# An attention and two feed-forward layers on one core: layer 2 as seven products of quarter matrices, and a list schedule with other matmul lengths

## The chip, the cores and the metric

The kernel runs on one core of one Trainium2 chip. Its time is device time in microseconds (us) for one execution, the median of the runs of one session. The engines are TensorE (PE, with its weight loads as PEld), VectorE (DVE), ScalarE (ACT), GpSimd (POOL) and the queue of SyncE (SP), which issues every DMA of this kernel. The trace comes from one profiled execution.

## The reference

Causal attention with a compressive memory gives 2304 tokens of 512 numbers; two feed-forward layers follow. All data are 32-bit floats.

```
x = attention(q, k, v, M_prev, z_prev, beta)          # 4 batches, 8 heads, 576 tokens, 64 wide
h = x @ moe_w_in;   r = max(h, 0)                     # 2304 x 512 by 512 x 2048
x = (s * r * r + b) @ moe_w_out                       # layer 1
h = x @ moe2_w_in
g = max(h, 0) + alpha * min(h, 0)
y = g @ moe2_w_out                                    # layer 2, 2304 x 512 out
```

## The kernel before

Every matrix product of the two layers is made exact enough by splitting both operands into a high and a low part: three matmuls (high by high, high by low, low by high) stand for one. Tokens are the moving operand, in blocks of 512 or 256 columns; the weights are the stationary operand, 128 by 128 each. Layer 1 has a block of 512 and seven of 256 columns, layer 2 four of 512 and one of 256. For each of 16 slices `f` of the hidden width, `g1` makes the hidden slice (12 matmuls into the bank `hb`, in layer 2 also `sp` and `ob`), ACT and DVE apply the activation and split the result (`gr`), and `g2` adds it to the output (12 matmuls into the four banks `yb`). A block has 16 x 24 = 384 matmuls. `evac` carries the output banks to DRAM (`y1` for layer 1, `out_t` for layer 2), and `load_x` loads and splits the input of the next block.

The weights lie in DRAM as 8-byte words. `weights` loads 512 KB for each of 32 halves of a layer, and DVE makes floats of them (three instructions, L870, L873, L876), ACT casts the high part (L879), DVE subtracts for the low part (L882). The weights of layer 2 are made while the last block of layer 1 and the first of layer 2 run, in place of those of layer 1.

The order of all instructions is made when the program is built. `Plan.order` is a list scheduler: each operation has an engine, a duration and a priority, and the operation that can start first on its engine is placed next. The chip then runs each engine's instructions strictly in that order, and waits by semaphores. The durations are functions of the size, such as `t_r` for one matmul of the layers (L286), `t_p` for scores, `t_dve` and `t_act`. Attention has the higher priority on PE; the matmuls of layer 1 fill what it leaves, and after attention has ended layer 1 has PE to itself.

## Time and profile before

| | |
|---|---|
| median of 3 runs | 980.5 us (980.23 to 982.16) |
| profiled execution, its own time | 980.97 us |
| span of the profiled execution | 978.9 us |
| PE busy | 962.6 us, 98% of the span |
| DVE busy, ACT busy | 602.4 us (62%), 471.5 us (48%) |
| bytes moved by DMA | 93.22 MB, mean 95 GB/s |

The span goes from the first to the last instruction; the time of the execution is 2.07 us more. Busy time on PE is modelled at its end, so the spacing of the starts of matmuls tells more than the busy share. Stages follow one another: attention with layer 1 between its pieces to about 422 us, layer 1 alone to about 585 us, its last matmuls mixed with the first of layer 2, then layer 2.

### The profile page before, as it was taken

The numbers are of one execution on the slowest core, as the hardware profiler recorded it, in microseconds if no ns is written. First come the engines' busy times: TensorE is split into PE (matmuls) and PEld (weight loads), VectorE is DVE, ScalarE is ACT, GpSimd is POOL, SyncE is SP. The second block draws the span as 40 slices with busy tenths as digits, with TensorE's granted clock in tenths as the row PEclk, the third lists the DMA queues.
The fourth block names the chain that finished last, engine by engine and source line by source line (L and its number), as shares of the span: only waits on it lengthen the run. The fifth ranks groups of instructions, "written<-read, shape, count | busy, mean of one in ns | idle before, by whom it ended". The sixth has DMA issues, their size and how long they took to land.

```text
span 978.9 us, 18001 instructions
## 1 busy us (share of the span) xinstructions
PE 962.6 (98%) x7068; PEld 828.7 (85%) x7068; DVE 602.4 (62%) x1471; ACT 471.5 (48%) x1183; POOL 5.3 (1%) x29
## 2 busy tenths in 40 slices
PE   7999999999999999999999999999999999999998
PEld 5777777788888888999999998888888888888898
DVE  7999998677776766542122999945434443534344
ACT  7877766787787777645454663212112111211111
POOL 1000000000000000000000000000000000000000
PEclk9999999999999999999999999999999999999999
DMA  5359955465657555641000755502000200100010
GB/s 176 100 161 239 243 197 155 111 163 115 151 117 155 137 121 104 120 164 55 1 23 10 224 170 158 162 1 86 1 1 11 65 1 1 44 1 0 1 45 22
DMA packets 114693, 93.22 MB, mean 95 GB/s; under 512 B 83377, under 2 KB 94641, under 8 KB 114609
## 3 DMA queue, kind: packets, MB, share of 16 engines
q1 hardware_dynamic: 114608, 92.08, 34.8%
q8 instruction: 55, 0.90, 0.4%
q14 instruction: 30, 0.24, 0.1%
HBM read 59.29 MB, written 13.11 MB: 74 GB/s over the span
## 4 chain that ended last, share of the span: by engine, by line
PE 89%; DVE 5%; ACT 4%; issue 1%; DMA 0%; SPq 0%; ACTq 0%; DVEq 0%
PE yb L973 13%; PE yb L975 13%; PE yb L974 13%; PE hb L932 9%; PE hb L934 8%; PE hb L933 8%; PE sp L932 3%; PE sp L934 3%; PE sp L933 3%; PE ob L775 2%; PE ob L932 2%; PE ob L934 2%; PE ob L933 2%; PE sp L775 2%; PE yb L775 2%; PE sp L679 1%
## 5 line engine op out<-in xcount | busy, mean ns | idle before, releaser
L973 PE MATMUL yb<-gr,wt 128*128 128x256 f32 (+2 forms) x832 | 270.7, 325 | 0.7 <-ACT gr L954 0.5
L975 PE MATMUL yb<-gr,wt 128*128 128x256 f32 (+2 forms) x832 | 268.3, 322 | 0.0
L974 PE MATMUL yb<-gr,wt 128*128 128x256 f32 (+2 forms) x832 | 267.6, 322 | 0.0
L932 PE MATMUL hb<-xr,wt 128*128 128x256 f32 (+1 forms) x592 | 183.9, 311 | 5.3 <-ACT gt L946 3.7
L934 PE MATMUL hb<-xr,wt 128*128 128x256 f32 (+1 forms) x592 | 179.1, 303 | 0.3 <-DVE wt L882 0.3
L933 PE MATMUL hb<-xr,wt 128*128 128x256 f32 (+1 forms) x592 | 179.1, 303 | 0.0
L973 PEld LDWEIGHTS yb<-gr,wt 128*128 128x128 f32 x832 | 156.4, 188 | 17.1 <-issue 2.5
L975 PEld LDWEIGHTS yb<-gr,wt 128*128 128x128 f32 x832 | 157.1, 189 | 13.9 <-DVE gr L955 1.1
L974 PEld LDWEIGHTS yb<-gr,wt 128*128 128x128 f32 x832 | 156.5, 188 | 12.2
L955 DVE TENSOR_TENSOR gr<-gt,gr 128x256 fp32r<-128x256 f32 (+1 forms) x168 | 84.1, 501 | 126.8 <-ACT gr L954 126.4
L954 ACT CAST gr<-gt 128x256 fp32r<-128x256 f32 (+1 forms) x168 | 78.7, 468 | 143.3 <-DVE gt L952 136.1
L932 PEld LDWEIGHTS hb<-xr,wt 128*128 128x128 f32 x592 | 111.3, 188 | 18.2 <-ACT gt L946 6.1
L934 PEld LDWEIGHTS hb<-xr,wt 128*128 128x128 f32 x592 | 111.8, 189 | 5.8 <-DVE wt L882 0.7
L933 PEld LDWEIGHTS hb<-xr,wt 128*128 128x128 f32 x592 | 111.3, 188 | 4.5
L946 ACT ACTIVATE gt<-hb 128x256 f32<-128x256 f32 (+1 forms) x128 | 52.6, 411 | 98.2 <-PE hb L934 94.1
L954 ACT CAST gr<-mz 128x512 fp32r<-128x512 f32 (+1 forms) x40 | 23.2, 579 | 154.0 <-DVE mz L952 153.9
L932 PE MATMUL sp<-xr,wt 128*128 128x512 f32 (+1 forms) x160 | 58.8, 367 | 0.0
L933 PE MATMUL sp<-xr,wt 128*128 128x512 f32 (+1 forms) x160 | 58.8, 367 | 0.0
L934 PE MATMUL sp<-xr,wt 128*128 128x512 f32 (+1 forms) x160 | 58.8, 367 | 0.0
L947 ACT ACTIVATE gt<-gt 128x256 f32<-128x256 f32 (+1 forms) x128 | 57.1, 446 | 2.5
L955 DVE TENSOR_TENSOR gr<-mz,gr 128x512 fp32r<-128x512 f32 (+1 forms) x40 | 25.6, 639 | 25.1 <-ACT gr L954 25.1
L949 DVE TENSOR_SCALAR mz<-ob,alv 128x512 f32<-128x512 f32 (+1 forms) x20 | 14.0, 698 | 37.8 <-PE ob L934 37.6
(343 smaller groups left out, 1484.7 us busy)
## 6 DMA issues: line engine op xcount, KB each, us to landing
pool<-wout SPq DMA_DIRECT2D x18, 512.0 KB, 4.3
pool<-win SPq DMA_DIRECT2D x16, 512.0 KB, 4.1
room<-wout SPq DMA_DIRECT2D x14, 512.0 KB, 3.9
room<-win SPq DMA_DIRECT2D x13, 512.0 KB, 4.2
pool<-y SPq DMA_DIRECT2D x18, 256.0 KB, 4.4
out_t<-pool SPq DMA_DIRECT2D x16, 256.0 KB, 2.1
y<-pool SPq DMA_DIRECT2D x22, 128.0 KB, 1.8
pool<-kp SPq DMA_DIRECT2D x9, 288.0 KB, 4.0
```

The lines of the kernel that those rows point to most:

```text
L775: T.matmul(bank_at(bk)[rows, x:x + n], half(sqp, odd, q0, nq), half(sk, odd, k0, n), start=True, stop=True, skip_group_check=True)
L932: T.matmul(H_, W_h, X_h, start=(d == 0), stop=False)
L933: T.matmul(H_, W_h, X_l, start=False, stop=False)
L934: T.matmul(H_, W_l, X_h, start=False, stop=(d == KD - 1))
L946: op("ACT", t_act(n, 50), lambda: A.activation(out=t_, in_=H_, func=AF.Relu), r=[hk, "gr"], w=[tk], prio=-1)
L947: op("ACT", t_act(n), lambda: A.activation(out=t_, in_=t_, func=AF.Square), w=[tk], prio=-1)
L949: op("DVE", t_dve(n, 1.04, 60), lambda: V.tensor_scalar(out=t_, in0=H_, scalar1=0.0, scalar2=alv[:, f:f + 1], op0=ALU.min, op1=ALU.mult), ...
L954: op("ACT", t_act(n), lambda: A.copy(out=G_h, in_=t_), r=[tk], w=[("gh", gj)], prio=-1)
L955: op("DVE", t_dve(n), lambda: V.tensor_tensor(out=G_l, in0=t_, in1=G_h.bitcast(F32), op=ALU.subtract), r=[tk, ("gh", gj)], w=[("gl", gj)], ...
L973: T.matmul(Y, W_h, G_h, start=first, stop=False, skip_group_check=True)
L974: T.matmul(Y, W_l, G_h, start=False, stop=False, skip_group_check=True)
L975: T.matmul(Y, W_h, G_l, start=False, stop=False, skip_group_check=True)
```

## The change

Layer 2 alone gets other mathematics. Tokens are cut in two halves (`NTH` = 1152), the inner width of each product in two, the outer width in two, so that each product is two-by-two quarters. Seven products of sums and differences of quarters replace the eight products of quarters. Products are numbered 1 to 7 in the code. They need sums of weight quarters, made once, sums of input quarters, made for each block, and sums of results.

- `prepare` (L1061, 16 times) loads two 512 KB pieces of layer 2's weights, makes floats (L1077, L1080, L1082, each twice), makes four differences of 256 columns (L1087) and stores seven matrices to DRAM (`wd`, 512 KB and 384 KB, L1090). All this stands where layer 1 runs alone. The key "words" lets the two loads of one `prepare` start only when the floats of the one ahead are made.
- `fetch` (L1093) loads these matrices back into the places of layer 1's weights (L1108) and splits them on ACT and DVE (L1110, L1112): those of the first product from the last block of layer 1 on, those of the second in the last third of the first product.
- `hidden` makes layer 2's first product for all tokens: three blocks of 2 x 384 columns by eight groups, each group with seven products of 6 matmuls (L1236 to L1238), three copies out of PSUM (`copy_out`, ACT), three sums (`join`, DVE, L1251), four activations (`leak`: ACT, then DVE, L1263) and four stores of 192 KB to DRAM (`g1`).
- `output` loads `g1` back (L1338) and makes the second product: in each of three blocks, seven products of four chunks of 12 matmuls (L1366 to L1368). For each chunk the operand is summed where the product asks for it (`sub`, DVE, L1199) and split (`split`: ACT L1193, DVE L1194) into one of three buffers.
- The scheduler's `t_r` becomes 115.5 ns up to 256 columns and (n + 32) / 2.4 above, `t_p` changes a little, and a PE operation of the layers after one of attention is given 130 ns more, the other way round 90 ns.

```diff
-BLOCKS = {1: [(0, 512)] + [(t, 256) for t in range(512, NT, 256)],
-          2: [(t, min(512, NT - t)) for t in range(0, NT, 512)]}
+BLOCKS = [(0, 512)] + [(t, 256) for t in range(512, NT, 256)]
...
+NS, NTH = 384, NT // 2
+GATE = 8
+GROUPS = [(b, f) for b in range(NTH // NS) for f in range(8)]
...
             if e == "PE":
+                layer = prio >= 10 ** 7
+                dur += 0 if layer == self.layer else 130.0 if layer else 90.0
+                self.layer = layer
...
-    return max(108.0, n / 2.4 + 2.5)
+    return 115.5 if n <= NB else (n + 32) / 2.4
+def t_s(n):
+    return 6 * (n + 32) / 2.4
...
-    return 200 + sum(186 + 4 * n / 2.4 for n in ns)
+    return 206 + 4 * sum(ns) / 2.4 + (0, 0, 4, 160, 364)[len(ns)]
...
+            for x, f in enumerate((fa, fb)):
+                s = Slot(RES["pw"], size=2)
+                op("SP", 475, lambda s=s, x=x: nc.sync.dma_start(out=at(s, 1024, I32), in_=src[i, x]),
+                   r=[("x1", B - 1, NP - 1, 1), "words"], w=[s], bytes_=524288)
...
+                    out=o(), in0=words(s, 1), scalar=-0x40000000, in1=o(), op0=ALU.bitwise_and, op1=ALU.bitwise_or), r=[s], w=[f] + ["words"] * x)
...
+            for out, in0, in1 in (((fa, 512), (fb, 0), (fa, 0)), ((fa, 768), (fb, 256), (fa, 512)),
+                                  ((fb, 512), (fb, 256), (fb, 0)), ((fb, 768), (fa, 256), (fa, 768))):
+                op("DVE", t_dve(256), lambda out=out, in0=in0, in1=in1: V.tensor_tensor(
+                    out=q(*out), in0=q(*in0), in1=q(*in1), op=ALU.subtract), r=[fa, fb], w=[out[0]])
+            for x, (f, a, n) in enumerate(((fa, 0, 4), (fb, 256, 3))):
+                op("SP", 475, lambda f=f, a=a, x=x, n=n: nc.sync.dma_start(
+                    out=wd[key][:, i, x, 0:256 * n], in_=q(f, a, 256 * n)), r=[f], w=[("wd", key, i, x)], bytes_=131072 * n)
...
+        def fetch(key, i):
...
+                op("ACT", t_act(256 * n), lambda s=s, x=x, a=a, n=n: A.copy(out=wp(i, x)[:, a:a + n, 0, :], in_=fold(see(s))),
+                   r=s.keys, w=[("w2", i, x, a)], prio=-0.8 if key == "wi" else -0.5)
...
+        def split(src, dst, prio):
+            act(dst, t_act(2 * NS), lambda: A.copy(out=see(dst, F32R, 0, 2 * NS), in_=see(src)), r=src.keys, prio=prio)
+            op("DVE", t_dve(2 * NS), lambda: V.tensor_tensor(
+                out=see(dst, F32R, 2 * NS, 2 * NS), in0=see(src), in1=see(dst, F32, 0, 2 * NS), op=ALU.subtract),
+               r=src.keys, w=dst.keys, prio=prio)
...
+        def product(P, g, bank):
+            b, f = GROUPS[g]
+            def mm():
+                for k in range(2):
+                    X_h, X_l = (see(XP[P], F32R, 2 * NS * lo + NS * k, NS) for lo in range(2))
+                    W_h, W_l = (weight(P, f, lo, k) for lo in range(2))
+                    o = bank_of[bank][:, 0:NS]
+                    T.matmul(o, W_h, X_h, start=(k == 0 and P in (1, 5, 2)), stop=False, skip_group_check=True)
+                    T.matmul(o, W_h, X_l, start=False, stop=False, skip_group_check=True)
+                    T.matmul(o, W_l, X_h, start=False, stop=False, skip_group_check=True)
...
+            for g, (b, f) in enumerate(GROUPS):
+                al, be, ga = bk(g)
+                p1, u2, p5 = (SIDE[3 * (g % 2) + x] for x in range(3))
+                product(1, g, al)
+                copy_out(al, p1)
+                product(5, g, ga)
+                copy_out(ga, p5)
+                if g > 0:
+                    last(g - 1)
+                if f == 0:
+                    split(RAW[3], XP[4], -3 if b else -0.7)
+                product(6, g, al)
+                copy_out(al, u2)
+                product(3, g, ga)
+                c = pick(RING)
+                join(ga, u2, c)
+                leak(g, 1, c, None, c)
+                product(2, g, be)
+                c = pick(RING)
+                join(be, p1, c)
+                leak(g, 0, c, None, c)
+                product(7, g, al)
+                c = pick(RING)
+                join(al, p5, c)
+                leak(g, 3, c, None, c)
...
+        def output():
+            U = [quarter(q) for q in range(4)]
+            ring = [Buf("gr", 0, 4 * NS)] + [Buf("xr", 4 * NS * i, 4 * NS) for i in range(2)]
+            side = FREE + [Buf("poolx", 4 * NS + NS * i, NS) for i in range(7)] + SIDE[0:3]
...
+                for P in (4, 5, 1, 2, 6, 3, 7):
+                    bank = names[{1: "a", 6: "a", 7: "a", 2: "b", 5: "c", 3: "c", 4: "d"}[P]]
+                    for m in range(4):
+                        a11, a12, a21, a22 = (U[q][m] for q in range(4))
+                        if P == 5:
+                            sub(a22, a21, a22, None, ALU.add)
+                        elif P == 6:
...
+                        src = {4: a22, 5: a22, 6: a22, 1: a11, 2: a12, 3: a12, 7: a21}[P]
+                        dst = ring[count[0] % len(ring)]
+                        count[0] += 1
+                        split(src, dst, None)
+                        def mm(P=P, m=m, dst=dst, bank=bank):
+                            for e in range(2):
...
+                                for j in range(2):
+                                    W_h, W_l = (weight(P, 2 * m + e, lo, j) for lo in range(2))
+                                    o = bank_of[bank[j]][:, 0:NS]
+                                    T.matmul(o, W_h, G_h, start=(m == e == 0 and P in (1, 2, 4, 5)), stop=False, skip_group_check=True)
+                                    T.matmul(o, W_l, G_h, start=False, stop=False, skip_group_check=True)
+                                    T.matmul(o, W_h, G_l, start=False, stop=False, skip_group_check=True)
```

DVE in the second part of layer 1, before the change: `gr` is the split of the hidden slice (L955), `xr` the next block's input (L1046), `yb` the output bank (L1008). These rows cover a little more than one block.

```order
L955 TENSOR_TENSOR gr<-gt,gr 128x256
L1046 TENSOR_TENSOR xr<-pool,xr 128x256 x2
L955 TENSOR_TENSOR gr<-gt,gr 128x256 x15
L1008 TENSOR_SCALAR pool<-yb_96,sbv 128x256
L1046 TENSOR_TENSOR xr<-pool,xr 128x256 x2
L1008 TENSOR_SCALAR pool<-yb_97,sbv 128x256
L955 TENSOR_TENSOR gr<-gt,gr 128x256
```

DVE in the same part of the program after the change: one whole `prepare` and the start of the next (`pool` and `poolx` hold the words, the floats and the differences; L944 is what L955 was).

```order
L1077 TENSOR_SCALAR poolx<-pool 128x512
L1080 SCALAR_TENSOR_TENSOR poolx<-pool,poolx 128x512
L1082 SCALAR_TENSOR_TENSOR poolx<-pool,poolx 128x512
L1077 TENSOR_SCALAR pool<-poolx 128x512
L1080 SCALAR_TENSOR_TENSOR pool<-poolx,pool 128x512
L944 TENSOR_TENSOR gr<-gt,gr 128x256
L1082 SCALAR_TENSOR_TENSOR pool<-poolx,pool 128x512
L1087 TENSOR_TENSOR poolx<-pool,poolx 128x256 x2
L1087 TENSOR_TENSOR pool<-pool 128x256
L944 TENSOR_TENSOR gr<-gt,gr 128x256
L1087 TENSOR_TENSOR pool<-poolx 128x256
L1077 TENSOR_SCALAR pool<-poolx 128x512
```

Where DVE had fifteen splits in a row, each split now stands behind instructions of a `prepare` that wait for loads; 45 of L944 stand between the first L1077 and the last L1087.

DVE at the end of layer 2 before the change: three instructions for each hidden slice of 512 columns.

```order
L949 TENSOR_SCALAR gt<-sp_102,alv 128x512
L952 SCALAR_TENSOR_TENSOR gt<-sp_102,gt 128x512
L955 TENSOR_TENSOR gr<-gt,gr 128x512
L949 TENSOR_SCALAR mz<-ob,alv 128x512
L952 SCALAR_TENSOR_TENSOR mz<-ob,mz 128x512
```

DVE in `output` after the change, products 5 and 6 of the first block (`spare` and `poolu` are quarters, `xr` and `gr` the three buffers).

```order
L1199 TENSOR_TENSOR spare<-poolu,spare 128x768 x2
L1194 TENSOR_TENSOR xr<-spare,xr 128x768
L1199 TENSOR_TENSOR spare<-poolu,spare 128x768
L1194 TENSOR_TENSOR xr<-spare,xr 128x768
L1199 TENSOR_TENSOR spare<-poolu,spare 128x768
L1194 TENSOR_TENSOR gr<-spare,gr 128x768
L1199 TENSOR_TENSOR spare<-spare,poolu 128x768
L1194 TENSOR_TENSOR xr<-spare,xr 128x768
```

The sum of the next chunk (L1199) stands ahead of the subtraction of this one (L1194), and so in the time in which ACT casts.

## Rows read from the trace of the kernel before

**Rows 1.** The page: busy time of the engines, and the granted TensorE clock in 40 slices.

```profile
PE 962.6 (98%) x7068; PEld 828.7 (85%) x7068; DVE 602.4 (62%) x1471; ACT 471.5 (48%) x1183; POOL 5.3 (1%) x29
PEclk9999999999999999999999999999999999999999
```

**Rows 2.** All that PE waited for: line, releaser, us in total, times, longest.

```profile
PE sp L775 <- DMA room<-kp: 4.4, 1, 4.4
PE hb L932 <- ACT gt L946: 3.7, 6, 1.4
PE hb L932 <- DVE xr L704: 1.6, 1, 1.6
PE yb L573 <- ACT pool L741: 0.7, 2, 0.4
```

**Rows 3.** Two stretches: us, PE, PEld, DVE, ACT, POOL busy, clock, DMA share, GB/s.

```profile
422.00:585.00 163.00, 162.53 (x1383) 161.27 (x1382) 75.12 (x157) 85.48 (x208) 0.00 (x0) 1.00 0.31 95
669.00:756.00 87.00, 87.00 (x385) 72.04 (x384) 37.99 (x55) 13.54 (x22) 0.00 (x0) 1.00 0.07 25
```

**Rows 4.** ACT in order of time: copies from PSUM that end a block.

```profile
447.53 0.48 ACT L1003 ACTIVATE pool<-yb,sbv 128x256 f32<-128x256 f32 x1 [0.21 <-DVE pool L1008]
491.36 0.48 ACT L1003 ACTIVATE pool<-yb,sbv 128x256 f32<-128x256 f32 x1 [0.21 <-DVE pool L1008]
...
669.17 0.59 ACT L1006 COPY pool<-yb 128x512 f32<-128x512 f32 x1 [2.66 <-PE yb L975]
756.21 0.59 ACT L1006 COPY pool<-yb 128x512 f32<-128x512 f32 x1 [2.67 <-PE yb L975]
...
930.34 0.59 ACT L1006 COPY pool<-yb 128x512 f32<-128x512 f32 x1 [0.47 <-PE yb L975]
975.10 0.37 ACT L1006 COPY pool<-yb 128x256 f32<-128x256 f32 x1 [0.32 <-PE yb L975]
```

**Rows 5.** PE in order of time: first and last of eight matmuls of 258 columns.

```profile
535.77 0.28 PE L974 MATMUL yb<-gr,wt 128*128 128x258 f32 x1
...
536.62 0.28 PE L975 MATMUL yb<-gr,wt 128*128 128x258 f32 x1
```

**Rows 6.** Weight loads of layer 2 in 700 to 900 us, one of twelve groups.

```profile
L973 PEld LDWEIGHTS yb<-gr,wt 128*128 128x128 f32 x148 | 27.8, 188 | 5.7
```

**Rows 7.** SP: the first two 512 KB loads of layer 2's weights; their time to landing.

```profile
425.37 0.41 SPq L867 DMA_DIRECT2D pool<-win  x1
...
425.87 0.38 SPq L867 DMA_DIRECT2D pool<-wout  x1
...
DMA to landing us min/median/max: 4.0/4.6/5.2
```

**Rows 8.** The same for L867 loads of `wout` over the whole program.

```profile
DMA to landing us min/median/max: 3.5/4.2/6.6
```

**Rows 9.** Groups of DVE and ACT by shape: count, busy us, mean ns.

```profile
L870 DVE TENSOR_SCALAR pool<-pool 128x512 int32<-128x512 int32 x33 | 13.7, 422 | 0.0
L873 DVE SCALAR_TENSOR_TENSOR pool<-pool 128x512 int32<-128x512 int32 x33 | 22.7, 689 | 0.4
L955 DVE TENSOR_TENSOR gr<-gt,gr 128x256 fp32r<-128x256 f32 x120 | 50.9, 424 | 106.8 <-ACT gr L954 106.4
L955 DVE TENSOR_TENSOR gr<-gt,gr 128x512 fp32r<-128x512 f32 x48 | 33.2, 691 | 20.0 <-ACT gr L954 20.0
L954 ACT CAST gr<-gt 128x256 fp32r<-128x256 f32 x120 | 48.8, 406 | 19.5 <-DVE gt L952 16.9 <-PE yb L974 0.2
L954 ACT CAST gr<-gt 128x512 fp32r<-128x512 f32 x48 | 29.9, 623 | 123.8 <-DVE gt L952 119.1 <-PE yb L974 3.7 <-PE yb L975 1.0
```

**Rows 10.** The end: the last matmul and the last copy out of PSUM.

```profile
975.13 0.28 PE L975 MATMUL yb<-gr,wt 128*128 128x256 f32 x1
975.44 0.43 DVE L1012 COPY pool<-yb 128x256 f32<-128x256 f32 x1 [0.25 <-PE yb L975]
```

More of the change, by code (lines that the diff above doesn't have):

```diff
@@ L978, in g2 @@
                    w=[yk, ("g2", f)] + ([(yslot[d], "y")] if d in yslot else []),
-                   prio=MOE + cm["m"] + (1.5 if layer == 1 and n == NBIG else 0))
+                   prio=MOE + cm["m"] + (1.5 if n == NBIG else 0))
             cm["m"] += 1
@@ L1010, in evac @@
                        r=yr + ["sbv"], w=[s], prio=-2)
-                else:
-                    op("DVE", t_dve(n), lambda s=s, Y=Y: V.tensor_copy(out=at(s, n), in_=Y), r=yr, w=[s], prio=-2)
-                dst = (y1 if layer == 1 else outT)[:, d, t0:t0 + n]
+                dst = y1[:, d, t0:t0 + n]
                 op("SP", 475, lambda s=s, dst=dst: nc.sync.dma_start(out=dst, in_=at(s, n)), r=[s],
@@ L1035, in load_x @@
                 op("SP", 475, lambda xr=xr, src=src: nc.sync.dma_start(out=xr(), in_=src), r=rk,
-                   w=[s] + [("xset", x) for x in ((0, 1, 3) if xs == 3 else (xs,))], bytes_=512 * step * n,
-                   prio=-2 if layer == 2 and blk > 0 else None)
+                   w=[s, ("xset", xs)], bytes_=512 * step * n)
                 for e in range(step):
@@ new lines, in ready, with weight, __init__ @@
+        def ready(P, i):
+            x, a = PLACE[P]
+            return ("w2", i, x, 0 if x else a // 2 * 2)
+        def weight(P, i, lo, k):
+            x, a = PLACE[P]
+            return wp(i, x)[:, a, lo, k * 128:(k + 1) * 128]
+        class Buf:
+            def __init__(self, region, c0, n):
+                self.region, self.c0, self.n = region, c0, n
+                key = "pool" if region in ("poolr", "poolu") else region
+                self.keys = [(key, c) for c in range(c0 // 128, (c0 + n + 127) // 128)]
@@ new lines, in build, with hold @@
+        seen = set()
+        def hold(buf):
+            claim, extra = [], []
+            for k in buf.keys:
+                if k in seen:
+                    continue
+                seen.add(k)
+                region, c = k
+                lo, hi = 128 * c, 128 * c + 127
+                if region == "pool":
+                    claim += range(NSLOT - XS)
+                elif region == "poolx":
+                    o = NSLOT - XS
+                    claim += range(o + lo // GW, o + hi // GW + 1)
+                elif region == "xr":
+                    extra += [("xset", int(hi >= 2 * KD * NB))]
+                elif isinstance(region, int):
+                    extra += wkeys("wi", 2 * region + 1) + wkeys("wo", 2 * region + 1)
+                elif region in ("gr", "gt"):
+                    extra += [(x, j) for x in (("gh", "gl") if region == "gr" else ("gt",)) for j in range(2)]
+            return sorted(set(claim)), list(dict.fromkeys(extra))
@@ new lines, in build, with act @@
+        every = [("wd", key, i, x) for key in ("wi", "wo") for i in range(8) for x in range(2)]
+        def act(buf, dur, fn, r=(), prio=None, eng="ACT", extra_w=(), bytes_=0):
+            claim, extra = hold(buf)
+            op(eng, dur, fn, r=list(r) + (every if claim else []) + ([("g2", GATE)] if buf in XP.values() else []) + (
+                [("y1", len(BLOCKS) - 1, d) for d in range(KD)] if claim and max(claim) > NSLOT - XS + 4 else []),
+               w=buf.keys + extra + list(extra_w), prio=prio, claim=claim, bytes_=bytes_)
@@ new lines, in hidden, with last @@
+        def hidden():
+            op("DVE", 90, lambda: V.tensor_scalar(out=alm, in0=alv, scalar1=-1.0, scalar2=1.0, op0=ALU.mult, op1=ALU.add),
+               r=["alv"], w=["alm"])
+            inputs(0)
+            ng = len(GROUPS)
+            bk = lambda g: (("S0", "H", ("Y", 0))[g % 3], ("O", ("Y", 2))[g % 2], ("S1", ("Y", 1))[g % 2])
+            parts = {}
+            def last(g):
+                al = bk(g)[0]
+                product(4, g, al)
+                leak(g, 2, None, al, pick(RING))
+                if GROUPS[g][0] == NTH // NS - 1:
+                    fetch("wo", GROUPS[g][1])
+            for g, (b, f) in enumerate(GROUPS):
[23 more added lines that the diff above has]
+                leak(g, 3, c, None, c)
+                if f == 7 and g + 1 < ng:
+                    inputs(b + 1)
+            last(ng - 1)
@@ L1086, in build @@
         for b in range(B):
             attention(b)
-        for i, (layer, blk) in enumerate((l, j) for l in (1, 2) for j in range(len(BLOCKS[l]))):
-            moe(layer, blk, i % 2 if layer == 1 else 2 + blk % 2)
+        for key, src in (("wi", win2), ("wo", wout2)):
+            for i in range(8):
+                prepare(src, key, i)
+        for blk in range(len(BLOCKS)):
+            moe(blk, blk % 2)
         flush()
+        hidden()
+        output()
         order = plan.order()
```

339 lines of the change are left out of this document (223 added, 116 removed).

## The prediction

> **What bounds the kernel now.** I first read the page's shares: PE is busy for 98% of the span, DVE for 62%, ACT for 48%, and the granted clock is full (2.4 GHz) in all 40 slices [rows 1]. Then what PE waited for: 4.4 us for the first load, 3.7 us six times for ACT, little else [rows 2]. So PE is the bound throughout, and a change is worth what it takes off PE, if nobody else becomes the bound. Last the stages: while layer 1 runs alone, DVE is busy for 75 of 163 us and DMA for 0.31; in a block of layer 2 DVE for 38 of 87 us and DMA for 0.07 [rows 3]. There is room beside PE.
>
> What counts is the spacing of PE's matmuls, not their modelled length. Two copies at the same place of consecutive blocks of 512 columns are 87.04 us apart [rows 4], over 384 matmuls 226.7 ns each. Matmuls of 258 columns start 0.85 us apart over seven gaps, 121 ns [rows 5]. Both are columns plus 32 at 2.4 GHz (226.7 and 120.8 ns), which is what the diff writes into the scheduler. A block of 256 columns takes 43.83 us in layer 1, 114 ns each, and 44.76 us at the end of layer 2, 117 ns [rows 4].
>
> **What PE is given.** Layer 2 before: four blocks at 87.04 us and one at 44.76 us make 392.9 us. After, the order holds 1008 matmuls of `hidden` and 1008 of `output`, all of 384 columns, in place of 1920. No row shows 384 columns. By 258 and 512 it is 416 columns at 2.4 GHz, 173.3 ns; a straight line between 117 ns at 256 and 226.7 at 512 gives 172 ns. I take 173.3, since two shapes above 256 agree on it: 2016 x 173.3 = 349.4 us, with 346.8 us as the lower end. That is 43.5 us less. The copies and sums beside it lie on ACT and DVE.
>
> A rule of the Trainium skill (Perfetto Trace Analysis, "Identifying the Most-Contended Engine") speaks against it: TensorE's headroom is to be judged by the busy share of LDWEIGHTS, not of matmuls. A load is busy for 188 ns [rows 6]; 2016 of them, if they could not overlap, would be 379.0 us, and 13.9 us would be gained, not 43.5. This case's trace does not bear it out: at 258 columns matmuls and their loads follow each other every 121 ns.
>
> **What DVE and ACT are given.** Prices by shape [rows 9]: DVE takes 424 ns for 256 and 691 ns for 512 columns, so 0.56 us for 384 and 0.96 us for 768; ACT's cast takes 406 and 623 ns, so 0.51 and 0.84 us. A group of `hidden` is 42 matmuls, 7.28 us of PE. It gives DVE three sums and four activations, 3.9 us, and ACT three copies and four activations, 3.6 us. In the last eight groups the fetch of the second weights adds 2.3 us to DVE and 2.1 to ACT: 6.2 and 5.7 of 7.28 us. In `output` a chunk is 12 matmuls, 2.08 us. Its subtraction takes DVE 0.96 us, with a sum 1.92 us. Over a block that is 44 x 0.96 + 8 x 0.56 = 46.7 of 58.2 us; in products 6, 3 and 7, which all need sums, 12 x 1.92 + 2 x 0.56 = 24.2 of 25.0 us. DVE stays below PE everywhere, at the closest place by 3%.
>
> **Terms that can hold PE up.**
>
> *Preparing weights, beside layer 1.* The order puts each split of the hidden slice on DVE (L944) behind instructions that wait for loads. In the order 45 splits stand within the 16 `prepare`; PE needs 43.83 / 16 = 2.74 us for each, so 123.3 us or 7.7 us per `prepare`. The chain of one `prepare` runs from load to load: the second load is issued 0.5 us after the first and lands 5.2 us later (a pair in the trace, behind 256 KB of other data) [rows 7], then 0.42 + 2 x 0.69 = 1.8 us of DVE [rows 9], some 0.2 us of semaphores: 7.7 us, or 8.1 with a split of 0.42 us inside. If the chain is the slower one, PE is held through L944, which `g2` needs. 16 x 0.4 is 6 us, nothing is the other end; I take 3 us. With the longest landing, 6.6 us [rows 8], the chain takes 9.1 us and the loss is 22 us: a rival.
>
> *From layer 1 to layer 2.* The first products' operands are split in the last half of the last block of layer 1, beside `fetch`. From there DVE has 11 x 0.96 us for sums and splits, eight fetches at 2.3 us and eight splits of layer 1 at 0.42 us: 33 us of work, of which the later fetches are not urgent, in 22 us of half a block and 7 us of a first group. I take 2 us, between 0 and 8.
>
> *Two changes of token block in `hidden`.* Each gives DVE 10.6 us more, in the 16.6 us between the first operand's release and the last one's use, in which 8.9 us of its usual work fall. Two of the sums can come earlier, 17.6 remain. About 1 us each, 2 us in all (0 to 6).
>
> *The last eight groups and the start of `output`*: the load of the next quarter waits for `hidden` to end and takes about 4 us, then 3 us of sum, cast and subtraction; product 4, which needs no such load, gives 8.3 us of PE work as cover. 2 us (0 to 8).
>
> *The end.* Now the last copy starts at 975.44 and the last matmul ends at 975.41 [rows 10]; 3.5 us are left from there to the end of the span. After, four sums of 0.56 us stand in line on one engine, two of them just ahead of the last matmul's end: 1.4 us more.
>
> *Attention and layer 1 under the new lengths.* After its last attention matmul the order keeps 1485 matmuls, 2016 of them taken off 3501; before it was 3288 less 1920, 1368. So attention ends 117 matmuls or 13 us of PE work sooner, and `prepare` begins sooner. PE waited little there, apart from the first load, so there is little to win; jitter in a new order can cost as much. Zero, between -5 and +6 us.
>
> **Sum.** 978.9 - 392.9 + 349.4 + 1.4 + (3 + 2 + 2 + 2) = 945.8 us of span, 2.07 us more in time (980.97 less 978.9): 947.9 us. The profiled execution lies 0.5 us above the median of the runs shown, so I predict **947 us**, 3.4% less than 980.5.
>
> **Rivals.**
>
> *More is won* (934 us or less). PE has no wait in layer 2 and loses some waits of layer 1: 947 less the 9 us of waits, less 5 us. For it: layer 2 runs without a wait now. Against: every stall above is a new one.
>
> *Others pace PE* (960 to 980 us). The `prepare` chain with late landings (22 in place of 3 us: 966 us), or layer 2's engines pushed out of step, in 24 groups 1 us each, 24 in place of 4: 967 us. For it: DVE and ACT run in a fixed order made from durations (`t_dve(512)` is 0.60 us) below those of the rows (0.69 us). Against: average load is well below PE's.
>
> *Weight loads bound layer 2*: 947 + 29.6 = 977 us.
>
> *Slower than before: the chunks of `output` run as a chain.* If sum, cast and subtraction of a chunk don't overlap with the next chunk's, it takes 0.96 + 0.84 + 0.96 + 0.3 = 3.06 us against PE's 2.08 us. With sums in 16 of 28 chunks, three blocks: 48 x 0.98 = 47 us, 994 us. It decides from 2.8 us a chunk on (48 x 0.7 = 34 us). Against it: the order has the next sum ahead of this subtraction, and there are three buffers.
>
> **How the numbers follow.** Forecast, 935 to 959 us: 0.74. More won: 0.04. Others pace PE: 0.15. Weight loads: 0.02. Slower by a chain: 0.04. The remaining 0.01 is no change. About 0.2% is what a measurement can tell here: faster 0.95, same 0.01, slower 0.04. The range of 934 to 966 us takes in the forecast, its unknown ends and the nearer half of the paced cases.
>
> **What would show it.** In the trace after: matmuls of 384 columns 173 ns apart; layer 2 some 355 us from its first to its last matmul; all waits of PE on DVE and ACT in layer 2 below some 8 us; L944 near its old rhythm of 2.74 us while L1077 runs; the last attention matmul near 409 us. The prediction is wrong if the spacing at 384 columns is 188 ns, if PE waits on L1194 chunk by chunk, if L944 comes late behind L1082, or if attention takes longer in its new order.

## The result, and the profile after

| | before | after |
|---|---|---|
| median of 4 runs each, one session | 980.92 us (980.23 to 982.16) | 941.03 us (938.19 to 942.06) |
| profiled execution, its own time | 980.97 us | 942.04 us |
| span of the profiled execution | 978.9 us | 940.0 us |

The ratio is 0.9587, with a 95% interval of 0.9562 to 0.9613: 4.1% less, where 3.4% was predicted. The predicted 947 us is 6 us too high and the range of 934 to 966 us holds the time.

First the page of the changed kernel, busy time and granted clock, which answers to [rows 1]. PE is as full as before, with DVE at 76% where it was at 62%.

```profile
PE 920.5 (98%) x7164; PEld 843.0 (90%) x7164; DVE 715.5 (76%) x1636; ACT 604.4 (64%) x1413; POOL 5.3 (1%) x29
...
PEclk9999999999999999999999999999999999999999
```

What PE waited for in the changed kernel, to be read beside [rows 2]. The three rows on L1368, L964 and L1236 are the new stalls; L796 and L928 are old ones under new line numbers.

```profile
PE sp L796 <- DMA room<-kp: 4.6, 1, 4.6
PE hb L928 <- ACT gt L941: 2.4, 3, 1.5
PE yb L1368 <- DVE xr L1194: 1.3, 1, 1.3
PE yb L964 <- DVE gr L944: 1.0, 5, 0.3
...
PE sp L1236 <- ACT waste L1248: 0.5, 1, 0.5
```

The stages (columns as in [rows 3]): the second part of layer 1, where `prepare` runs, then `hidden` without its first groups, then `output`.

```profile
422.00:536.00 114.00, 113.63 (x987) 113.24 (x986) 88.03 (x194) 53.43 (x136) 0.00 (x0) 1.00 0.78 274
...
590.00:760.80 170.80, 169.82 (x973) 168.00 (x972) 130.61 (x220) 109.36 (x217) 0.00 (x0) 1.00 0.54 175
760.80:935.50 174.70, 173.27 (x998) 172.61 (x996) 129.78 (x154) 78.38 (x106) 0.00 (x0) 1.00 0.41 125
```

DVE and the DMA queue are far busier than before: 0.78 of DMA in 422 to 536 us, where [rows 3] has 0.31. PE is still idle for about 1 us only in `hidden` and 1.4 us in `output`.

PE in order of time, from the changed kernel: two matmuls 24 apart in layer 1, the one long wait of `output`, two matmuls 59 apart at 384 columns (59 x 173.2 ns), and the last one.

```profile
464.42 0.28 PE L928 MATMUL hb<-xr,wt 128*128 128x256 f32 x1
...
467.14 0.28 PE L928 MATMUL hb<-xr,wt 128*128 128x256 f32 x1
...
769.46 0.34 PE L1367 MATMUL yb<-xr,wp 128*128 128x384 f32 x1
771.12 0.44 PE L1368 MATMUL yb<-xr,wp 128*128 128x384 f32 x1 [1.32 <-DVE xr L1194]
...
839.72 0.33 PE L1367 MATMUL sp<-xr,wp 128*128 128x384 f32 x1
...
849.94 0.33 PE L1366 MATMUL ob<-xr,wp 128*128 128x384 f32 x1
...
935.05 0.34 PE L1368 MATMUL sp<-xr,wp 128*128 128x384 f32 x1
```

ACT's copies at the ends of layer 1's blocks, which answer to [rows 4] (447.53 and 491.36 there).

```profile
447.21 0.46 ACT L991 ACTIVATE pool<-yb,sbv 128x256 f32<-128x256 f32 x1
...
491.20 0.46 ACT L991 ACTIVATE pool<-yb,sbv 128x256 f32<-128x256 f32 x1
...
536.24 0.48 ACT L991 ACTIVATE poolx<-yb,sbv 128x256 f32<-128x256 f32 x1
```

So the blocks of layer 1 end where they did, with all of `prepare` beside them: a block takes 43.99 us where it took 43.83. From the copy at 536.24 us to the end of the span it is 403.8 us; before it was 442.6 us (978.9 less 536.28, the same copy of before). All of the gain lies there.

The weight loads of `hidden` and `output`, one of many groups, as in [rows 6]: 188 ns each.

```profile
L1236 PEld LDWEIGHTS yb<-poolr,wp 128*128 128x128 f32 x96 | 18.0, 188 | 0.6 <-DVE poolx L1251 0.6
```

DVE in order of time: a sum of `output` that waits for a load, with the three instructions behind it, and the sums at the end.

```profile
769.24 0.96 DVE L1199 TENSOR_TENSOR spare<-poolu,spare 128x768 f32<-128x768 f32 x1 [1.88 <-DMA poolu<-g]
770.11 0.95 DVE L1194 TENSOR_TENSOR xr<-spare,xr 128x768 fp32r<-128x768 f32 x1
770.98 0.95 DVE L1199 TENSOR_TENSOR spare<-poolu,spare 128x768 f32<-128x768 f32 x1
771.85 0.95 DVE L1194 TENSOR_TENSOR gr<-spare,gr 128x768 fp32r<-128x768 f32 x1
...
934.90 1.02 DVE L1251 TENSOR_TENSOR gr<-sp,waste 128x384 f32<-128x384 f32 x2 [4.07 <-PE sp L1368]
935.84 0.55 DVE L1251 TENSOR_TENSOR gt<-sp,waste 128x384 f32<-128x384 f32 x1
936.30 0.55 DVE L1251 TENSOR_TENSOR waste<-sp,waste 128x384 f32<-128x384 f32 x1
```

Two things are to be seen here. The first four are 0.95 us long but start 0.87 us apart: independent DVE instructions overlap by 0.08 us. And from the last matmul's end (935.39 us) to the end of the span it is 4.6 us, where it was 3.5 us.

### The profile page after: what moved, and what is told of

It reads as the page before. It is cut to its first block, busy times and chain, and to the rows that moved or that the text cites. A ratio compares the mean times of both kernels' runs of the same rounds, so it can differ in the third digit from the quotient of the medians.

```text
span 940.0 us, 19297 instructions
## 1 busy us (share of the span) xinstructions
PE 920.5 (98%) x7164; PEld 843.0 (90%) x7164; DVE 715.5 (76%) x1636; ACT 604.4 (64%) x1413; POOL 5.3 (1%) x29
## 4 chain that ended last, share of the span: by engine, by line
PE 74%; DVE 13%; ACT 5%; DMA 5%; issue 2%; SPq 0%; DVEq 0%; ACTq 0%
PE yb L962 6%; PE yb L964 5%; PE hb L928 5%; PE yb L963 5%; PE hb L929 5%; PE hb L930 5%; PE sp L1368 3%; PE sp L1367 3%; PE sp L1366 3%; PE yb L1368 2%; PE yb L1367 2%; PE yb L1366 2%; PE yb L1236 2%; PE yb L1238 2%; PE yb L1237 2%
## 5 line engine op out<-in xcount | busy, mean ns | idle before, releaser
L928 PE MATMUL hb<-xr,wt 128*128 128x256 f32 (+1 forms) x512 | 152.5, 298 | 2.5 <-ACT gt L941 2.4
L962 PE MATMUL yb<-gr,wt 128*128 128x256 f32 (+2 forms) x512 | 154.1, 301 | 0.7 <-ACT gr L943 0.5
L964 PE MATMUL yb<-gr,wt 128*128 128x256 f32 (+2 forms) x512 | 151.2, 295 | 1.0 <-DVE gr L944 1.0
L930 PE MATMUL hb<-xr,wt 128*128 128x256 f32 (+1 forms) x512 | 149.4, 292 | 0.3 <-DVE wt L894 0.3
L929 PE MATMUL hb<-xr,wt 128*128 128x256 f32 (+1 forms) x512 | 149.3, 292 | 0.0
L928 PEld LDWEIGHTS hb<-xr,wt 128*128 128x128 f32 x512 | 96.3, 188 | 11.6 <-issue 4.4
L962 PEld LDWEIGHTS yb<-gr,wt 128*128 128x128 f32 x512 | 96.4, 188 | 9.1 <-issue 3.7
L964 PEld LDWEIGHTS yb<-gr,wt 128*128 128x128 f32 x512 | 96.6, 189 | 5.9 <-DVE gr L944 2.9
L944 DVE TENSOR_TENSOR gr<-gt,gr 128x256 fp32r<-128x256 f32 (+1 forms) x128 | 58.3, 456 | 56.2 <-ACT gr L943 53.7
L930 PEld LDWEIGHTS hb<-xr,wt 128*128 128x128 f32 x512 | 96.4, 188 | 3.5 <-DVE wt L894 0.7
L929 PEld LDWEIGHTS hb<-xr,wt 128*128 128x128 f32 x512 | 96.2, 188 | 2.1
L963 PE MATMUL yb<-gr,wt 128*128 128x256 f32 (+2 forms) x320 | 93.6, 292 | 0.0
L963 PEld LDWEIGHTS yb<-gr,wt 128*128 128x128 f32 x320 | 60.3, 188 | 1.2
L963 PE MATMUL yb<-gr,wu 128*128 128x256 f32 (+2 forms) x192 | 56.2, 292 | 0.0
L1262 ACT ACTIVATE waste<-poolx 128x384 f32<-128x384 f32 x48 | 25.2, 525 | 26.2 <-DVE poolx L1251 26.1
L1193 ACT CAST xr<-spare 128x768 fp32r<-128x768 f32 x30 | 25.0, 835 | 24.7 <-PE sp L1367 7.5
L963 PEld LDWEIGHTS yb<-gr,wu 128*128 128x128 f32 x192 | 36.2, 188 | 0.9
L1193 ACT CAST xr<-poolu 128x768 fp32r<-128x768 f32 x24 | 20.1, 838 | 25.1 <-PE sp L1367 13.8
L1236 PE MATMUL yb<-poolr,wp 128*128 128x384 f32 x104 | 35.0, 336 | 0.4 <-DVE poolx L1251 0.3
```

The source lines that it names most:

```text
L928: T.matmul(H_, W_h, X_h, start=(d == 0), stop=False)
L929: T.matmul(H_, W_h, X_l, start=False, stop=False)
L930: T.matmul(H_, W_l, X_h, start=False, stop=(d == KD - 1))
L944: op("DVE", t_dve(n), lambda: V.tensor_tensor(out=G_l, in0=t_, in1=G_h.bitcast(F32), op=ALU.subtract), r=[tk, ("gh", gj)], w=[("gl", gj)], ...
L962: T.matmul(Y, W_h, G_h, start=first, stop=False, skip_group_check=True)
L963: T.matmul(Y, W_l, G_h, start=False, stop=False, skip_group_check=True)
```

## The experiments

The theory to be tested: PE's columns make the gain, the new work stays beside PE, the lengths of the schedule are worth nothing. The rivals: the lengths give a part; DVE, the chain of `prepare` or the chunks of `output` pace PE; weight loads bound it. Each time below is a median beside the kernel before (980.5 to 981.8 us in the three sessions), with the ratio's 95% interval; the changed kernel's ratio is 0.9587.

### The lengths of the schedule

**All old, in the changed kernel.**

```diff
-                layer = prio >= 10 ** 7
-                dur += 0 if layer == self.layer else 130.0 if layer else 90.0
-                self.layer = layer
...
-    return 115.5 if n <= NB else (n + 32) / 2.4
+    return max(108.0, n / 2.4 + 2.5)
...
-    return 6 * (n + 32) / 2.4
+    return 6 * (n / 2.4 + 2.5)
...
-    return 206 + 4 * sum(ns) / 2.4 + (0, 0, 4, 160, 364)[len(ns)]
+    return 200 + sum(186 + 4 * n / 2.4 for n in ns)
```

> The changed kernel, scheduled with the old lengths of matmuls and no price for a change of kind; its work is the same. My theory: the gain is the columns that PE no longer has in layer 2, the lengths are worth nothing, so 941 us with 3 us either way, and attention still ends near 408 us, since layer 1's place among the pieces of attention is set by how many matmuls fit. Rival: the lengths brought a part of the 40 us, because DVE and ACT are given an order that PE's real pace upsets: then 947 us or more, with waits of PE on DVE or ACT of several us that the changed kernel does not have.

954.4 us (0.9713 to 0.9753). My theory fell, the rival's number came. The copy that ended layer 1's block 6 at 536.24 us starts at 542.14 us, and in the first group of layer 2 PE has one wait of 7.5 us on L1260, which is L1263 under other numbers.

**New lengths alone, in the kernel before.** The same edits, the other way round, without layer 2's products.

> The kernel before, with the new lengths and prices of changes alone. My theory: 981 us with 3 us either way. Rival (the lengths give a part of the gain by themselves): 976 us or less. If the lengths only help where the new layer 2 has a dense order on DVE and ACT, this run shows nothing and the run with the old lengths in the changed kernel does.

985.72 us (1.0043 to 1.0069), 5 us slower than before, with block 6's copy at 543.97 us. So the lengths are no better in themselves. They help only in the changed kernel, and two more runs asked which of them.

**Only the products' length old.**

```diff
-    return 6 * (n + 32) / 2.4
+    return 6 * (n / 2.4 + 2.5)
```

> The changed kernel with only the length of layer 2's own products put back to the old form (162.5 in place of 173.3 ns a matmul). The run with all lengths old was 13 us slower than the changed kernel: 6 us by the end of layer 1 and one wait of 7.5 us in the first group of layer 2, where DVE had the splits of fetched weights (L1112) ahead of an activation (L1263). In this kernel's order those splits still stand ahead of the first group, as in the changed kernel. My theory now: the lengths of layer 1 and of scores set how far the loads and splits are when layer 2 begins, and the length of layer 2's products does not matter: 941 us with 3 us either way. Rival (the products' own length makes the wait): 947 to 950 us, with a wait of several us on L1263.

939.64 us (0.9562 to 0.9596), no wait above 1 us in layer 2.

**Only the lengths of layer 1 and of scores old**, and no price for changes of kind.

```diff
-                layer = prio >= 10 ** 7
+                layer = False
...
-    return 115.5 if n <= NB else (n + 32) / 2.4
+    return max(108.0, n / 2.4 + 2.5)
...
-    return 206 + 4 * sum(ns) / 2.4 + (0, 0, 4, 160, 364)[len(ns)]
+    return 200 + sum(186 + 4 * n / 2.4 for n in ns)
```

> The other half: the changed kernel with the old lengths of layer 1's matmuls and of scores and no price for changes of kind, the products of layer 2 at their new length. Its order has ten splits of fetched weights behind the first sums of the first group, as in the run with all lengths old. My theory: the whole 13 us are here, block 6 of layer 1 ends near 542 us, PE waits some 7 us on L1263 in the first group and the granted clock falls behind it: 954 us with 3 us either way. Rival: 947 us or less.

954.84 us (0.9719 to 0.9758): the whole difference is here. DVE of this run in the first groups of layer 2 (L1112 splits fetched weights, L1263 is the activation of product 4):

```profile
611.23 0.96 DVE L1112 TENSOR_TENSOR wp<-poolx,wp 128x768 fp32r<-128x768 f32 x1 [2.00 <-ACT wp L1110]
612.50 1.35 DVE L1112 TENSOR_TENSOR wp<-poolx,wp 128x512 fp32r<-128x512 f32 x2 [0.32 <-ACT wp L1110]
613.89 0.61 DVE L1263 SCALAR_TENSOR_TENSOR poolx<-poolx,alm,sp 128x384 f32<-128x384 f32 x1
```

PE at the same place:

```profile
608.65 0.34 PE L1238 MATMUL ob<-poolr,wp 128*128 128x384 f32 x1
614.56 0.69 PE L1236 MATMUL sp<-xr,wp 128*128 128x384 f32 x1 [5.57 <-DVE poolx L1263]
```

And the stages of this run around it (columns as in [rows 3]):

```profile
609.00:617.00 8.00, 2.29 (x6) 1.78 (x6) 3.74 (x6) 3.24 (x5) 0.00 (x0) 0.78 0.63 205
617.00:625.00 8.00, 6.97 (x25) 6.98 (x26) 7.36 (x14) 5.25 (x12) 0.00 (x0) 0.58 0.35 124
```

DVE reaches the splits of weights that are just being fetched, waits for them, and the activation that frees PE's bank stands behind them. PE starts 31 matmuls in 16 us where 92 fit: 5.7 us are idle, and the granted clock is 0.58 in the 8 us that follow. In the changed kernel all but one of the 24 splits stand ahead of the first sums of layer 2 (L1251), beside layer 1; here eleven stand behind them.

What moved them is the end of attention, since `prepare` waits for its last output, and the fetch of the first product's weights for the last store of `prepare`. Here are the first loads of `prepare` (L1074) and all of these fetches (L1108) with the times of the first and the last start, ahead of the dots in the changed kernel, behind them in this run:

```profile
L1074 SPq DMA_DIRECT2D pool<-win x10: 332/429/838, 409.5 to 463.0; - x10
L1108 SPq DMA_DIRECT2D poolx<-wdwi x24: 319/320/531, 544.0 to 592.9; - x24
...
L1074 SPq DMA_DIRECT2D poolx<-win x5: 345/383/923, 424.0 to 472.0; - x5
L1108 SPq DMA_DIRECT2D poolx<-wdwi x24: 319/320/829, 564.8 to 613.2; - x24
```

The fetch begins 20.8 us later, though the last matmul of layer 1 starts only 3.9 us later. Of the 20.8 us, 6.3 are a longer `prepare`, and the rest is attention, whose last matmul starts at 422.7 us in place of 408.3. Behind it 1404 matmuls of layer 1 are left here and 1485 in the changed kernel: the planner, which with the old lengths takes 109 in place of 115.5 ns for one, set 81 more, some 9 us, among the pieces of attention. The numbers left go the same way elsewhere: 1368 in the kernel before and 1482 in it with the new lengths, and 1509 in the next run, where 117 in place of 115.5 ns is all that changes. The other 5 us are waits of PE at L594, which transposes the rows of attention's softmax: 5.5 us in all in the first 64 us, where the changed kernel has 0.4 us. The longest:

```profile
PE yb L594 <- ACT room L579: 2.1, 1, 2.1
```

By spans, 4.7 us are lost by block 6's copy (540.94 us), about what these waits take, and 7.8 us behind it. Which of the three (matmuls, scores, changes of kind) does how much of it was not tried, though the next run shows that the length of the matmuls alone moves the number left; nor is it known why the old lengths make the planner's order wait at L594.

**A length 1.5 ns longer.**

```diff
-    return 115.5 if n <= NB else (n + 32) / 2.4
+    return 117.0 if n <= NB else (n + 32) / 2.4
```

> The changed kernel with 117.0 in place of 115.5 ns for a matmul of up to 256 columns, both within what the trace shows (113 to 118). My theory: the place of attention's end and of layer 1's blocks moves by a few us with any change of these numbers, without a sense of direction (block 6 ended at 536.3, 544.0, 542.1 and 536.2 us in the kernel before, in it with the new lengths, in the changed kernel with the old ones, and in the changed kernel): 938 to 949 us, with the difference at block 6's end, and no wait of several us in layer 2. Rival (the better the length, the better the order, so that 1.5 ns make nothing): 941 us with 1.5 us either way, block 6 at 536 us.

942.67 us (0.9592 to 0.9622), block 6's copy at 538.85 us: inconclusive. Of its 2.6 us, 2.0 lie in one block (48.85 us in place of 46.81), whose matmuls start 117.9 ns apart from 425 us on, where those of the changed kernel start 113.3 ns apart. A run below shows that a block can take 1.6 us more in this way without any change of order.

### What could pace PE

**`prepare` without its key.**

```diff
-                   r=[("x1", B - 1, NP - 1, 1), "words"], w=[s], bytes_=524288)
+                   r=[("x1", B - 1, NP - 1, 1)], w=[s], bytes_=524288)
...
-                    out=o(), in0=words(s, 1), scalar=-0x40000000, in1=o(), op0=ALU.bitwise_and, op1=ALU.bitwise_or), r=[s], w=[f] + ["words"] * x)
+                    out=o(), in0=words(s, 1), scalar=-0x40000000, in1=o(), op0=ALU.bitwise_and, op1=ALU.bitwise_or), r=[s], w=[f])
```

> The changed kernel without the key that lets the two loads of a piece of weights start only when the floats of the piece ahead are made. The first L1077 and the last L1087 of the changed kernel lie 128 us apart, 8.0 us for each of 16 pieces, which is what the prediction worked out for the chain of loads; but DVE's idle time there stands before the split of the hidden slice and is put down to ACT's cast, not to a load. My theory: PE leads and the chain has room, so nothing changes: 941 us with 2 us either way, and the blocks of layer 1 keep 44.0 us. Rival: the chain of loads paces PE there, and blocks come down to 43.8 us or attention's place moves: 2 to 4 us less.

939.15 us (0.9564 to 0.9590), not to be told from the changed kernel. The block that took 43.99 us takes 43.98 us. The loads now crowd each other (median 6.3 us to landing, where the changed kernel has 5.1 us) and DVE still hardly waits for them. For the changed kernel the view of L1074, those loads, says:

```profile
  DVE pool L1077: 1.1, 1
...
DMA to landing us min/median/max: 3.5/5.1/7.7
```

One wait of 1.1 us for 32 loads: the chain does not pace PE.

**`output` without its cover.**

```diff
-                for q in (3, 2, 0, 1):
+                for q in (0, 3, 2, 1):
...
-                for P in (4, 5, 1, 2, 6, 3, 7):
+                for P in (1, 4, 5, 2, 6, 3, 7):
```

> The changed kernel with the products of the output in the order 1, 4, 5, 2, 6, 3, 7 and the quarter of product 1 loaded first: the first product now needs a quarter whose place comes free only when the first product of layer 2 ends, where product 4, which has its quarter already, stood ahead. My theory: PE idles for one load (3.3 us to landing), cast, subtraction and semaphores (2.1 us), and some more for later chunks, whose loads share the queue: 6 to 8 us, 948 us. In the second and third block the places come free early enough. Rival: the load is hidden anyway or the planner covers it otherwise: 941 us; or it returns in every block: 956 us or more.

950.64 us (0.9684 to 0.9711), 9.6 us more, a little over the forecast. PE of this run at the place:

```profile
759.28 0.34 PE L1238 MATMUL yb<-poolr,wp 128*128 128x384 f32 x1
764.35 0.69 PE L1366 MATMUL sp<-gr,wp 128*128 128x384 f32 x1 [4.74 <-ACT gr L1193]
```

and the stretch behind it:

```profile
764.00:768.00 4.00, 3.65 (x10) 3.15 (x11) 1.92 (x2) 1.64 (x3) 0.00 (x0) 0.50 1.05 379
```

4.9 us without a matmul, then a granted clock of 0.50 (the level of 1.2 GHz) for 4 us, which costs 2 us more, and one wait of 0.7 us at the start of each later block. The cover of product 4 is real.

**Two buffers in `output`.**

```diff
-            ring = [Buf("gr", 0, 4 * NS)] + [Buf("xr", 4 * NS * i, 4 * NS) for i in range(2)]
+            ring = [Buf("xr", 4 * NS * i, 4 * NS) for i in range(2)]
```

> The changed kernel with two buffers for the split operands of the output in place of three. A chunk's cast can then start only when PE has left the chunk two ahead, and PE has one chunk (12 matmuls of 173 ns, 2.08 us) until it needs it. My theory: cast 0.84, next sum on DVE 0.96, subtraction 0.96 and semaphores 0.3 us make 2.1 us without a sum and 2.2 to 2.3 us with one, in 48 of 84 chunks: 4 to 10 us more, 948 us, as many short waits of PE on L1194. Rival (the chain of a chunk runs serially even with three buffers, as the prediction's slow rival has it, and is hidden only by the third buffer): 3.06 against 2.08 us in 48 chunks, 40 us or more, 985 us. If the buffers don't matter: 941 us.

950.23 us (0.9656 to 0.9696), 9.2 us more, at the upper end of the theory and far from the serial chain. Of these, 1.75 us are there at block 6's copy (537.99 us), and come from one block of layer 1 at 117.9 in place of 113.3 ns a matmul. PE's waits in `output` of this run:

```profile
PE yb L1368 <- DVE xr L1194: 4.3, 7, 1.0
PE sp L1368 <- DVE xr L1194: 0.6, 2, 0.3
```

**The subtractions of `output` twice.**

```diff
                         split(src, dst, None)
+                        op("DVE", t_dve(2 * NS), lambda src=src, dst=dst: V.tensor_tensor(
+                            out=see(dst, F32R, 2 * NS, 2 * NS), in0=see(src), in1=see(dst, F32, 0, 2 * NS), op=ALU.subtract),
+                           r=src.keys, w=dst.keys)
```

> The changed kernel with each subtraction of the output (L1194) made twice, to the same place. It adds 84 x 0.96 us to DVE and nothing to PE. My theory (DVE stays below PE in the output by 3% where it is closest): in the 16 chunks of a block with a sum DVE then needs 2.88 us against PE's 2.08 us, and PE waits for the difference: 16 x 0.8 + 8 x 0.56 of sums of results, 13 to 17 us a block, 45 us in all, 986 us. Rival (DVE has much more room there, so that the prediction's account of it is wrong): 941 to 960 us. If the granted clock falls at the waits, more than 986 us.

967.06 us (0.9823 to 0.9861), 26 us more, where 45 were expected: my price of DVE was too high. The middle block of `output` in this run (columns as before; DVE is 66.83 of 67.00 us busy):

```profile
825.00:892.00 67.00, 60.99 (x339) 58.11 (x338) 66.83 (x81) 27.03 (x37) 0.00 (x0) 1.00 0.39 120
```

DVE is the bound here without a gap, so the block's length is DVE's price: 72 instructions of 768 columns at 0.87 us and 8 sums at 0.47 us make 66.4 us. The rows read 0.95 us for one, which would make 72.9 us. The pace of starts counts, not the length of the row.

**288 columns.** `NS` is 288, with four blocks of tokens, and every buffer stays where it is at 384.

```diff
-NS, NTH = 384, NT // 2
+NS, NW, NTH = 288, 384, NT // 2
...
-        XP = {P: Buf("poolr", 4 * NS * i, 4 * NS) for i, P in enumerate((5, 6, 3, 2, 4))}
+        XP = {P: Buf("poolr", 4 * NW * i, 4 * NS) for i, P in enumerate((5, 6, 3, 2, 4))}
...
```

> The changed kernel with four token blocks of 2 x 288 columns in place of three of 2 x 384, buffers at the same places: 2688 matmuls in place of 2016. My theory (columns plus 32 at 2.4 GHz): 133.3 ns each, 358.4 us in place of 349.4, 9 us more; DVE then needs 5.7 of a group's 5.6 us in the last eight groups and 19.1 of 19.2 us in three products of the output, which can cost 1 to 5 us: 951 to 955 us. Rival (a weight load of 188 ns bounds each matmul where it is longer): 188 ns apart, 505 us, 1095 us. If the price were a fixed time per column alone: 941 us.

958.48 us (0.9735 to 0.9775), 17.5 us more. PE of this run, two matmuls 77 apart, 132.6 ns each:

```profile
839.71 0.29 PE L1366 MATMUL ob<-xr,wp 128*128 128x288 f32 x1
...
849.92 0.29 PE L1368 MATMUL sp<-xr,wp 128*128 128x288 f32 x1
```

Columns plus 32 at 2.4 GHz (133.3 ns) holds at a fourth size, beside 258, 384 and 512, and a load of 187 ns does not bound a matmul every 133 ns. 9 of the 17.5 us are the columns, 4.3 us the place of block 6's copy (540.52 us), the rest waits at the blocks' changes and at the start of `output`; my 951 to 955 us left the middle one out.

### Versions meant to be better

**Late loads, and bank after bank in the last chunk.**

```diff
-                for q in (3, 2, 0, 1):
+                def load(q):
...
+                for q in (3, 2) if b == 0 else (3, 2, 0, 1):
+                    load(q)
...
+                            if b == 0 and m == 2:
+                                op("SP", 475, lambda u=a22: nc.sync.dma_start(out=late, in_=see(u)[:, 0:1]), r=a22.keys, bytes_=512)
+                                load(0)
+                                load(1)
...
-                            for e in range(2):
+                            for j, e in [(j, e) for j in range(2) for e in range(2)] if m == 3 and P == 7 else [(j, e) for e in range(2) for j in range(2)]:
...
```

> A version meant to be better: in the first block of the output the loads of the quarters of products 1 and 2 wait until the third sum of product 5 is made (a store of one column stands ahead of them on the queue), and in the last chunk of all the matmuls of one bank come ahead of those of the other. My theory: the wait of 1.3 us at the start of the output comes from twelve loads issued together that share the queue (median 7.9 us to landing, where the prediction took 4 us), and goes; the sums of the first bank no longer stand behind the last matmul, which saves 1 us of the 4.6 us from the last matmul to the end: 2 us less in all, 939 us. Rival: the late loads hold product 1 (a wait on L1194 or L1193 some 8 us later), 941 us or more.

940.04 us (0.9556 to 0.9589). The long wait is gone (0.3 us left in `output`), and from the last matmul's end to the end it is 4.0 in place of 4.6 us; the median can't be told from the changed kernel's 941.03 us. Its profiled execution lost 1.6 us in one block of layer 1, though the order there is the same. PE of this run at the place of the two matmuls shown at 464.42 and 467.14 us for the changed kernel:

```profile
465.12 0.28 PE L928 MATMUL hb<-xr,wt 128*128 128x256 f32 x1
...
467.94 0.28 PE L928 MATMUL hb<-xr,wt 128*128 128x256 f32 x1
```

24 matmuls take 2.82 us here and 2.72 us there, with no wait in either.

**The same without the key of `prepare`.**

```diff
-                   r=[("x1", B - 1, NP - 1, 1), "words"], w=[s], bytes_=524288)
+                   r=[("x1", B - 1, NP - 1, 1)], w=[s], bytes_=524288)
...
```

> The version with late loads and bank after bank at the end, and without the key between pieces of weights. Each of the two was within 2 us of the changed kernel by itself; the one took 1.3 us of waiting and 0.6 us of the end away, the other nothing that a row shows. My theory: 938 us, 3 us less than the changed kernel, as far as the pace of layer 1's 256-column matmuls lets it be seen, which is 113.3 ns in one block and 117.7 ns in the same block of another run. Rival: 941 us.

940.58 us (0.9576 to 0.9605): not faster. From block 6's copy to the end of the span, the runs whose layer 2 has no long wait take 400.7 us (no key), 400.7 (late loads), 400.4 (old length of products), 400.6 (117 ns) and 401.8 us (this one); the changed kernel's profiled execution takes 403.8 us. Its wait of 1.3 us in `output` is 0.3 us in the run without the key, and the runs with the old length of products and with 117 ns show none; its two changes of token block cost 2.0 us, and 0.7 us in the run without the key. So these stalls are not the same in every run, and there was little to win. No version beat the changed kernel by more than can be measured.

## Why the prediction was right, and where its sizes were wrong

The path that the prediction named is the one that the runs show: PE's columns make the gain, and the new work on DVE, ACT and the queue stays beside PE. The sizes of the other terms were off, and one zero came out right for a reason that the prediction does not give.

**What PE is given** was right to the row: 173.2 ns at 384 columns, where 173.3 was taken, so 43.5 us less. The rival of weight loads fell in the same rows. The Trainium skill (Perfetto Trace Analysis, "Identifying the Most-Contended Engine") judges TensorE's headroom by MFU, the share of the peak rate that a kernel's matmuls reach, and by the busy share of LDWEIGHTS. The prediction named the second alone, and the rival made of it a time for each matmul. Here that share is as good as full at 173 ns a matmul (168.0 of 170.8 us in `hidden`) and at 133 ns (69.39 of 70.00 us from 780 us on with 288 columns), so it does not tell how close together matmuls can start.

**Preparing weights** (3 us) was the term most over-sized: the two whole blocks beside it lost 0.16 and 0.12 us (43.99 and 45.04 us, against 43.83 and 44.92 us of before). What did not come is the condition "If the chain is the slower one, PE is held". The period of 7.7 to 8.1 us was right (the loads go out from 409.5 to 527.6 us, 7.9 us for each piece), but DVE waited for a load once. And without the key the time did not change. DVE's idle time ahead of the splits L944 goes to ACT's cast, which follows PE's own pace. Count, busy time and idle time of most of them, from 425 to 527 us:

```profile
L944 DVE TENSOR_TENSOR gr<-gt,gr 128x256 fp32r<-128x256 f32 x37 | 15.7, 423 | 16.0 <-ACT gr L943 15.7
```

**The other stalls** were taken at 6 us. By the starts of PE's matmuls beyond 173.3 ns, the start of `output` costs 1.6 us, the two changes of token block 2.0 us together and the first groups of layer 2 0.5 us, 4.1 us. The span leaves 3.5 us for all of it. That it is not more is luck in part: in the last block of layer 1, 24 matmuls take 2.72 us in this execution (543.44 to 546.16 us) and 2.82 us in the profiled one of before (543.77 to 546.59 us), two paces that come and go without a change of order (see the end), and over a block they differ by up to 1.6 us. The load at the start of `output` was priced at about 4 us; ten such loads of 384 KB share the queue, and their median to landing is 7.9 us. The cover of 8.3 us held it nearly: 1.3 us of waiting, and 9.6 us without the cover.

**DVE below PE "by 3%"** came from rows read one by one. At the pace of starts, products 6, 3 and 7 need 12 x 1.74 + 2 x 0.47 = 21.8 of 25.0 us. DVE had more room than the prediction thought, and the rival of paced engines came nowhere near; with the subtractions doubled it is the bound.

**Attention and layer 1 under the new lengths**, zero, was right in the net: the copies stand within 0.3 us of [rows 4] and the last attention matmul is at 408.3 us. But the lengths are not worth zero: the old ones would have cost the changed kernel 13.8 us (954.84 against 941.03 us). The prediction counted the 117 matmuls by which attention ends sooner and saw that `prepare` begins sooner, but looked for a win in PE's waits of attention alone ("so there is little to win"). What the sooner start buys is that the weights of layer 2 are split when it begins. Of the 12.5 us between the spans, 4.7 lie in this term, near its end of 6 us, and 7.8 behind it, where "From layer 1 to layer 2" would have come out at its end of 8 us; beside the four runs that need some 400.6 us there it is 11 us. The prediction priced that term from the finished order and did not ask which numbers made it safe. New lengths in the old kernel cost 5 us.

**The end** was 1.1 us more, where 1.4 was taken.

The sum with these terms is 978.9 - 43.5 + 1.1 + 3.5 = 940.0 us, the profiled span, with 0.0 for layer 1 (0.3 us gained in its beginning, 0.3 us lost beside `prepare`). The 3.5 us are taken from the span itself, so the sum tests the other terms only together.

## What to carry to other kernels

Price PE by the spacing of starts at the shape in question, and DVE by the spacing of starts in a dense stretch; row lengths overstate both. In a list schedule the lengths matter where one engine's order mixes loads that are still under way with work that another engine waits for, so look there for what a planner's error would do. Ask too what a chain of loads waits for before it can start: here a length that is some 6% short put more of layer 1 ahead of attention's end, and all that waits for that end came later. Ask what a stall costs with the clock behind it. Before work on a stall of 1 or 2 us, look whether other runs have it too.

## What the runs showed of the hardware

Matmuls of 256 columns run at one of two steady paces, 113.3 or 117.7 ns (2.72 and 2.82 us for 24), mostly for a whole block, in the same order of instructions and at a granted clock of 1.00; columns plus 32 at 2.4 GHz, which holds above 256, would be 120 ns. A block so takes 1.6 us more or less, as much as many of the medians here differ by. In the run with late loads the blocks on either side kept the pace of the changed kernel; in the run that also lacks the key the pace went from 112.9 to 117.5 ns within a block, between 453 and 464 us. What decides it is open.

Behind 4.9, 5.7 and 7.6 us without a matmul the granted clock was 0.50 for 4 us, 0.58 for 8 us and 0.53 for 8 us (no cover, layer 1's lengths old, all lengths old). Behind the wait of 1.3 us in the changed kernel it did not fall: all its windows stand at 1.00.

Independent DVE instructions of 768 columns started 0.87 us apart, though each lasts 0.95 us. The Trainium skill (VectorE: DVE Perf Modes, "The DRAIN you can't avoid") has the next op wait until the pipe is empty, and says that one which is not held starts earlier. These rows agree with the second.
